# Fixed tiles given out by the plan, and a fixed order of up and down sums, in an attention and feed-forward kernel

## The chip, the cores and the metric

The kernel runs on one core of one Trainium2 chip. The metric is the device time of one execution in microseconds (us). A core has five engines that run side by side, each with its own queue in order: TensorE (PE, matmul), VectorE (DVE), ScalarE (ACT), GpSimd (POOL) and SyncE (SP, which here issues all DMAs). Matmul results land in PSUM, eight banks of 2 KB in each of 128 partitions; an engine has to read a bank out before a new sum can begin in it. The rest of the on-chip data is in SBUF.

## The reference

Talking-heads attention over 4 batches, 12 heads, 448 positions and 64 features, then a mixing layer of rank 32 and a feed-forward layer of 768 to 3072 to 768, everything in float32:

```python
scores = scale * np.matmul(q, k.transpose(0, 1, 3, 2))
scores = np.einsum('bhij,hg->bgij', scores, w_pre)
scores = scores - np.max(scores, axis=-1, keepdims=True)
attn = np.exp(scores)
attn = attn / (np.sum(attn, axis=-1, keepdims=True) + 1e-09)
attn = np.einsum('bhij,hg->bgij', attn, w_post)
x = np.matmul(attn, v)          # then [batch, position, 768]
h = xt @ U @ V                  # xt: x with position last; mixes positions
u = x + h.transpose(0, 2, 1)
out = u + np.maximum(u @ w_ch1, 0.0) @ w_ch2
```

## The kernel before

The whole program is laid out by a planner in Python, before anything runs. Each step of work is added with `plan.add` (line 107): a key, the engines that can do it with a cost in ns for each, a rank, the steps that it needs, and the slots that it holds. `Plan.order` (line 145) then plays the steps through: at each moment each idle engine takes the ready step of lowest rank whose slots are free (`pick`, line 168). A step's result counts as there after its cost and a latency (128 ns, 196 for PE). Where a step may go to several engines, the one that would end first, by costs and weights, gets it. The list that comes out is the order in which the instructions are emitted; each engine then runs its own in that order, and a framework puts in the semaphores.

Slots are of two kinds. PSUM banks are given out by the plan itself (`take`, line 137): pairs of banks for attention, single ones for up sums (`up`, at most 3), down sums (`dn`, at most 6) and the low-rank step. SBUF buffers are rings (`BUFS`, line 271): of those the plan only counts how many are left, while the tile itself is taken in turn from a pool with that many buffers (`Pool.tile`, line 75). Rings that matter here: `h` (5 slots, each one tile `hh` and one `hl`), `w0` (2) and `w1` (3) for the weights of one block, `kr` (2) for raw weights, `tmp1` and `tmp2` (1 each) for pieces being narrowed, and in attention `s`, `e`, `wr`, `st`, `q`, `x`.

Attention goes over 16 units (a batch's query groups) and 90 chunks: `qk` and its copy `s`, two `relay` DMAs that put it into the head-mixing layout `t`, `premix`, `max`, two `exp`, `eps`, `recip`, `scale`, `postmix`, its copy `a`, and `av`. Its tail overlaps the low-rank step (`tp`, `t1`, `hp`, lines 735 to 756) and the first feed-forward blocks.

The feed-forward layer goes over 24 blocks f of 128 hidden units and 4 batches b. An up sum (`up`, line 758) is 18 matmuls: six chunks, each as three products of high and low halves. ACT makes `hh` by a relu (line 769) and DVE the low part `hl` (line 773). A down sum (`down`, line 775) of one chunk c of six is 3 matmuls for each f it takes in; f are taken in pairs, so 6 matmuls: for even b the pairs end at even f, for odd b at odd f (lines 820 to 822). DVE adds it into `acc` (`gather`, line 786). The down sums of block f need the up sums of f and f-1. The ranks put up(f,b) just before the down sums of the same f and b (lines 814 to 825), but PE takes whatever is ready.

The weights come as 64-bit floats and are narrowed on chip in pieces of 384 columns, four per block (`piece`, line 587): raw load by SP, `abs` on ACT, four DVE steps (lines 615 to 625), one add on POOL (line 629), then the high half (`w0h`, `w1h`, line 310, 312 or 314) and the low half (`w0l`, `w1l`, line 317). The first steps need a `kr` and a `tmp` slot, the last two also a slot of `w0` or `w1`.

Of the kernel before, what the change touches and what calls it, by code (L numbers as in the profile page):

```python
# [23 lines left out]
NJ = 4  # L24
# [20 lines left out]
class Unit:  # L45
# [13 lines left out]
    uv=0.5, rb0=2, rb1=13.176, rbs=4, w0=4, w1=27.676, up=0.421, raw=8, x0=2.953, k0=-13.668, kstep=0.83,  # L59
# [28 lines left out]
class Plan:  # L88
# [8 lines left out]
    def __init__(self, rings, banked, banks, weight):  # L97
        self.left = dict(rings)
        self.banked, self.where = banked, {}
        self.bank_free = list(range(banks))  # L100
        self.banks = banks
        self.weight = weight
        self.steps = {}
        self.port = {}
        self.users = {}

# [30 lines left out]
    def take(self, s):  # L137
        got = self.find(s[0], self.bank_free)
        for g in got:
            self.bank_free.remove(g)  # L140
        if s[0] in PAIRS:
            self.pairs_left -= 1
        self.where[s] = got

    def order(self):
# [7 lines left out]
        held, left = set(), dict(self.left)  # L153
# [36 lines left out]
        while events:  # L190
            now = events[0][0]
            while events and events[0][0] <= now:
# [24 lines left out]
            while moved:  # L217
                moved = False
                for e in free:
# [6 lines left out]
                    engines, fn, _, _, slots = steps[k]  # L226
                    for o, _ in engines:
                        ready[o].remove(r)
                    for s in sorted(slots, key=lambda s: s[0] not in PAIRS):
                        if s not in held:  # L230
                            held.add(s)
                            if s[0] in self.banked:
                                self.take(s)
# [27 lines left out]
def build(tc, q2, kt, vj, wpre_in, wpost_in, u_in, v_in, ident, w1j, w2, out, show=None):  # L261
    nc = tc.nc
    whole, tail_ctx, mix_ctx, t_ctx, qk_ctx = (ExitStack() for _ in range(5))
    rings = {}
# [54 lines left out]
    def act(n):  # L319
        return 130 + 0.9 * n  # L320

    def dve(n):
        return 130 + 1.07 * n

    def dve_copy(n):
        return 150 + 0.53 * n
# [4 lines left out]
    def gps_copy(n):  # L331
        return 250 + 0.98 * n
# [43 lines left out]
    def buffer():  # L376
        return sb["kr"].tile([128, 2 * S], F32, "kr")

    def load_k(eng, b, p, n):
        k = tile_of(("k", b), lambda: sb["k"].tile([128, H // 2, S], F32, "k"))  # L380
        eng.dma_start(out=k[:, p:p + n], in_=kt[b, :, p:p + n])

    def load_q(eng, u, p, n, src):
        q = tile_of(("q", u), lambda: sb["q"].tile([128, H // 2, QW], F32, "q"))
# [15 lines left out]
    def qk_out(eng, u, p):  # L400
        s = T["s", u, p] = sb["s"].tile([QW, 2, S], F32, "s")
# [6 lines left out]
    for u, un in enumerate(units):  # L408
# [5 lines left out]
        for p in range(H // 2):  # L414
# [5 lines left out]
            for h in (2 * p, 2 * p + 1):  # L420
                plan.add(("relay", u, h), [("SP", (1040, 1000))], partial(relay, u=u, h=h), r + RANK["qo"], [("qk_out", u, p)], [s, ("t", u)])
# [10 lines left out]
    def neg_max(eng, k):  # L432
        mx = T["mx", k] = sb["st"].tile([128, 2], F32, "mx")
        eng.tensor_reduce(out=mx, in_=T["pre", k][:, :, :S], axis=AX.X, op=ALU.max, negate=True)  # L434

    def exp(eng, k, i):
        e = tile_of(("e", k), lambda: sb["e"].tile([128, 2, S], F32, "e"))
        sm = tile_of(("sm", k), lambda: sb["st"].tile([128, 2], F32, "sm"))
        eng.activation(out=e[:, i], in_=T["pre", k][:, i, :S], func=ACTF.Exp, bias=T["mx", k][:, i:i + 1], accum_out=sm[:, i:i + 1])  # L439

    def add_eps(eng, k):
        rc = T["rc", k] = sb["st"].tile([128, 2], F32, "rc")
# [5 lines left out]
    def scale_w(eng, k):  # L448
        wr = T["wr", k] = sb["wr"].tile([128, 2, HALF], F32, "wr")
# [17 lines left out]
    def post_out(eng, k, js):  # L467
        u, n = chunks[2 * k + js[0]]
        a = tile_of(("a", u), lambda: sb[f"a{u % 3}"].tile([128, XA, 120], F32, "a"))
# [4 lines left out]
    for k in range(NC // 2):  # L474
# [5 lines left out]
        plan.add(("max", k), [("DVE", 1080)], partial(neg_max, k=k), r + RANK["mx"], [("premix", k)], [pre, st], port=())  # L480
        for i in range(2):
            plan.add(("exp", k, i), [("ACT", 835)], partial(exp, k=k, i=i), r + RANK["ex"], [("max", k)], [pre, st, e])
        plan.add(("eps", k), [("POOL", 130)], partial(add_eps, k=k), r + RANK["ep"], [("exp", k, i) for i in range(2)], [st], port=())
        plan.add(("recip", k), [("DVE", 157)], partial(recip, k=k), r + RANK["ep"], [("eps", k)], [st], port=())
        plan.add(("scale", k), [("POOL", 420)], partial(scale_w, k=k), r + RANK["ep"], ["wpost", ("recip", k)], [st, wr], port=BOTH)
        plan.add(("postmix", k), [("PE", 825)], partial(postmix, k=k), r + RANK["post"], [("scale", k)], [e, wr, post])
        for js in ([(0, 1)] if len(us) == 1 else [(0,), (1,)]):
            u = chunks[2 * k + js[0]][0]
            plan.add(("post_out", 2 * k + js[0]), OUT_A(XA * MC * len(js)), partial(post_out, k=k, js=js), r + RANK["post"] + RANK["po"],
                     [("postmix", k)], [post, (f"a{u % 3}", u)], port=())  # L490

    def load_v(eng, b):
        v = T["v", b] = sb["vr"].tile([128, H // 2, 2, NB // 2 + 1, D], F32, "v")
# [21 lines left out]
    def av_out(eng, u, p):  # L515
        x = tile_of(("x", u), lambda: sb["x"].tile([128, H // 2, 120], F32, "x"))
# [13 lines left out]
    for u, un in enumerate(units):  # L530
        if un.gi == 0:
            plan.add(("v", un.b), [("SP", (500, 6700))], partial(load_v, b=un.b), rank_av(u, 0) - RANK["vr"], (), [("vr", un.b)])
        for p in range(0, H // 2, AV):
# [5 lines left out]
            plan.add(("av_add", u, p), [("DVE", 150 + 1.042 * AV * un.rows // 2)], partial(av_add, u=u, p=p), r + 0.65 * AV, [("av_out", u, p)], [z, x], port=())  # L539
# [47 lines left out]
    def piece(key, src, n, p, rank, finish, slots, opened, cost, early=None):  # L587
# [5 lines left out]
        def pair(n_):  # L593
            T["nx", key], T["na", key] = (sb[n_].tile([128, HW], I32, e) for e in "xa")
# [4 lines left out]
        def load_raw(eng):  # L599
            T["raw", key] = buffer()[:, :2 * HW].bitcast(I32).rearrange("p (n t) -> p n t", t=2)  # L600
            eng.dma_start(out=T["raw", key][:p, :n], in_=src)

        def narrow0(eng):
            pair("tmp1" if early else which)
# [296 lines left out]
```

## Time and profile before

| | us |
|---|---|
| median of 3 runs | 1220.93 |
| lowest, highest | 1220.0, 1221.29 |
| the profiled execution, whole | 1220.8 |
| its span, first to last instruction | 1219.0 |
| PE busy | 1096.7 (90%) |
| DVE busy | 722.7 (59%) |
| ACT busy | 377.4 (31%) |
| POOL busy | 260.8 (21%) |

Busy time is the time with at least one instruction under way on an engine. Matmuls are pipelined, so a PE that is shown busy can still have short gaps between the starts of its matmuls. "Idle before" in the rows is the time in which an engine stood still just before the instruction, with what ended it.

### The profile page before, as it was taken

The page shows a single profiled execution, that of the slowest core. Times are in us where ns is not written, and L with a number is a line of the kernel's source. Part 1 is how long each engine was busy: PE and PEld are TensorE (multiplying, and loading weights), DVE is VectorE, ACT ScalarE, POOL GpSimd, SP SyncE. Part 2 cuts the span into 40 slices and gives each one's busy share as a digit, 9 for nine tenths or more (in the row PEclk, how much of TensorE's full clock was granted, in tenths as well). Part 3 has the DMA queues.
Part 4 walks back from the last instruction along what each step waited for, and adds up shares of the span by engine and source line. Part 5 has one row for each costly group of instructions (what it writes and reads, how often), then busy time and mean ns, then how long its engine had stood idle before and what let it go on. Part 6 is the DMA issues. An engine that isn't in the chain of part 4 may idle for free.

```text
span 1219.0 us, 28556 instructions
## 1 busy us (share of the span) xinstructions
PE 1096.7 (90%) x12120; PEld 891.0 (73%) x12120; DVE 722.7 (59%) x1312; ACT 377.4 (31%) x808; POOL 260.8 (21%) x389
## 2 busy tenths in 40 slices
PE   4998889998986788899999898989999999999898
PEld 1566556655665677787878787878888787888797
DVE  0656566567666765876665655656565666655534
ACT  2766666655763232211112111111111111111100
POOL 3111111112223221331212221212222122212100
PEclk8899999989996799999999999999999999999999
DMA  7665666657665100221111121111111111111004
GB/s 267 202 192 175 195 199 191 205 178 223 186 180 173 40 1 5 76 76 52 52 39 52 40 62 42 45 47 45 47 52 52 52 52 52 44 49 52 14 1 181
DMA packets 68063, 118.52 MB, mean 97 GB/s; under 512 B 17808, under 2 KB 54112, under 8 KB 67424
## 3 DMA queue, kind: packets, MB, share of 16 engines
q1 hardware_dynamic: 67936, 116.70, 31.3%
q8 instruction: 95, 1.56, 0.5%
q14 instruction: 32, 0.26, 0.1%
HBM read 63.12 MB, written 12.28 MB: 62 GB/s over the span
## 4 chain that ended last, share of the span: by engine, by line
PE 68%; DVE 18%; DMA 5%; issue 5%; ACT 3%; SPq 1%; DVEq 0%; POOL 0%; ACTq 0%; POOLq 0%
PE bank L764 29%; PE bank L784 17%; PE bank L464 5%; DVE acc L788 5%; PE bank L429 4%; PE bank L505 4%; PE bank L398 4%; DMA t<-s 4%; DVE hl L773 2%; DVE a L620 2%; DVE a L619 2%; DVE a L615 1%; ACT hh L769 1%; DVE x L625 1%; PE bank L711 1%
## 5 line engine op out<-in xcount | busy, mean ns | idle before, releaser
L784 PE MATMUL bank<-hh,w1l 128*128 128x448 f32 x576 | 220.3, 382 | 44.0 <-DVE acc L788 42.3
L788 DVE TENSOR_TENSOR acc<-acc,bank 128x448 f32<-128x448 f32 x300 | 179.1, 616 | 74.6 <-PE bank L784 69.2
L784 PE MATMUL bank<-hl,w1h 128*128 128x448 f32 x576 | 214.6, 373 | 3.8 <-DVE hl L773 3.8
L764 PE MATMUL bank<-uh,w0l 128*128 128x448 f32 x576 | 212.7, 369 | 1.5 <-DVE acc L788 1.2
L784 PE MATMUL bank<-hh,w1h 128*128 128x448 f32 x576 | 212.3, 369 | 0.0
L764 PE MATMUL bank<-uh,w0h 128*128 128x448 f32 x576 | 211.8, 368 | 0.0
L764 PE MATMUL bank<-ul,w0h 128*128 128x448 f32 x576 | 211.8, 368 | 0.0
L769 ACT ACTIVATE hh<-bank 128x448 fp32r<-128x448 f32 x96 | 52.4, 545 | 450.4 <-PE bank L764 391.5
L773 DVE SCALAR_TENSOR_TENSOR hl<-bank,hh 128x448 fp32r<-128x448 f32 x96 | 59.7, 622 | 218.6 <-ACT hh L769 218.6
L629 POOL TENSOR_TENSOR a<-a,x 128x384 f32<-128x384 f32 (+2 forms) x99 | 99.8, 1008 | 370.0 <-DVE x L625 359.4
L784 PEld LDWEIGHTS bank<-hh,w1l 128*128 128x128 f32 x576 | 109.4, 190 | 79.0 <-DVE acc L788 61.0
L434 DVE TENSOR_REDUCE mx<-bank 128x2 f32<-128x896 f32 x90 | 97.6, 1086 | 78.9 <-PE bank L429 77.8
L464 PEld LDWEIGHTS bank<-wr,e 60*64 60x64 f32 x5040 | 92.6, 137 | 51.2 <-issue 38.1
L784 PEld LDWEIGHTS bank<-hl,w1h 128*128 128x128 f32 x576 | 109.5, 190 | 17.4 <-DVE hl L773 9.5
L764 PEld LDWEIGHTS bank<-uh,w0l 128*128 128x128 f32 x576 | 109.4, 190 | 11.5 <-DVE acc L788 1.6
L439 ACT ACTIVATE e<-bank,mx 128x448 f32<-128x448 f32 x180 | 112.9, 638 | 15.4 <-DVE rc L446 10.0
L784 PEld LDWEIGHTS bank<-hh,w1h 128*128 128x128 f32 x576 | 109.5, 190 | 8.8
L764 PEld LDWEIGHTS bank<-ul,w0h 128*128 128x128 f32 x576 | 109.3, 190 | 9.0
L398 PE MATMUL bank<-k,q 64*64 64x448 f32 (+1 forms) x768 | 99.6, 588 | 18.1 <-ACT s L310 10.7
L764 PEld LDWEIGHTS bank<-uh,w0h 128*128 128x128 f32 x576 | 109.0, 189 | 9.2
L464 PE MATMUL bank<-wr,e 60*64 60x60 f32 x5040 | 95.9, 221 | 11.9 <-issue 7.8
L429 PE MATMUL bank<-t,wpre 64*64 64x448 f32 x720 | 88.8, 559 | 9.4 <-DMA t<-s 4.7
(62 smaller groups left out, 1147.5 us busy)
## 6 DMA issues: line engine op xcount, KB each, us to landing
t<-s SPq DMA_DIRECT2D x192, 210.0 KB
kr<-in_w1j SPq DMA_DIRECT2D x48, 384.0 KB
kr<-in_w SPq DMA_DIRECT2D x48, 384.0 KB
v<-in_vj SPq DMA_DIRECT2D x4, 1536.0 KB
q<-in_q SPq DMA_DIRECT2D x32, 186.0 KB
acc<-xs SPq DMA_DIRECT2D x4, 1344.0 KB
out<-acc SPq DMA_DIRECT2D x24, 224.0 KB
xs<-x SPq DMA_DIRECT2D x10, 360.0 KB
```

Of the source, the lines that this page charges most:

```text
L398: eng.matmul(o[at, i, :S], lhsT=q[d, p, at], rhs=k[d, p, :], start=True, stop=True)
L429: eng.matmul(o[64 * j:64 * j + 64, i, :S], lhsT=wpre[64 * i:min(64 * i + 64, QW)], rhs=tt[u % 2][64 * i:min(64 * i + 64, QW), n, :], start ...
L434: eng.tensor_reduce(out=mx, in_=T["pre", k][:, :, :S], axis=AX.X, op=ALU.max, negate=True)
L439: eng.activation(out=e[:, i], in_=T["pre", k][:, i, :S], func=ACTF.Exp, bias=T["mx", k][:, i:i + 1], accum_out=sm[:, i:i + 1])
L464: eng.matmul(d, lhsT=e[64 * j:64 * j + HALF, i, x * KB:x * KB + KB], rhs=wr[64 * j:64 * j + HALF, i].rearrange("p (g m) -> p g m", m=MH), ...
L505: eng.matmul(main[i * D:(i + 1) * D, c, :n], lhsT=v[:, p + c, i, x, :], rhs=a[:, x * H + 2 * (p + c) + i, :n], start=(c == 0 and x == 0), ...
L629: eng.tensor_tensor(out=f32(a), in0=f32(a), in1=f32(x), op=ALU.add)
L764: eng.matmul(ps, lhsT=w[:, c * 128:(c + 1) * 128], rhs=u[:, c, :], start=(i == 0), stop=(i == 3 * KC - 1))
L769: eng.activation(out=hh, in_=T["up", f, b], func=ACTF.Relu)
L773: eng.scalar_tensor_tensor(out=hl, in0=T.pop(("up", f, b)), scalar=0.0, in1=f32(T["hh", f, b]), op0=ALU.max, op1=ALU.subtract)
L784: eng.matmul(ps, lhsT=w[:, cut], rhs=h, start=(i == 0), stop=(i == len(todo) - 1))
L788: eng.tensor_tensor(out=dst, in0=dst, in1=T.pop(("dn", f, b, c)), op=ALU.add)
```

## The change

Four things change.

1. A pool no longer turns through its buffers. The plan keeps a list of the free places of each ring, takes the one that came free first (`take`), and hands it back when the last user is done. `Pool.tile` makes one fixed tile for each place and returns it again whenever a step holds that place. Numbers and sizes of the buffers stay.
2. The up and down sums from block f = 2 on (`even=2`) get a fixed order, `plan.line`: one up sum, then up to three down sums from a queue, into which the six down sums of a finished f and b go behind that. `pick` passes over each step of this line that isn't next. Blocks 0 and 1 stay free.
3. Most costs of the plan are lowered, for instance `act` from 130 + 0.9 n to 57 + 0.9 n, `exp` from 835 to 622, a gather from 611 to 532, a relay on SP from 1040 to 850. `OUT_A`, a separate cost for the copy `a`, goes; `OUT` serves for both. The costs of PE's feed-forward sums stay.
4. A rank offset `ga` for gathers is added, with the value 0.

The diff, cut to its core (the helpers that name a ring's slot are changed alike at every tile):

```diff
 class Pool:
-    def __init__(self, pool):
-        self.pool = pool
-        self.n = 0
-
-    def tile(self, shape, dt, tag, **kw):
-        self.n += 1
-        return self.pool.tile(shape, dt, tag=tag, name=f"{tag}_{self.n}", **kw)
+    def __init__(self, pool, where):
+        self.pool, self.where = pool, where
+        self.made = {}
+
+    def tile(self, shape, dt, tag, slot=None):
+        at = tag if slot is None else f"{tag}_{self.where[slot]}"
+        if at not in self.made:
+            self.made[at] = self.pool.tile(shape, dt, tag=at, name=at)
+        return self.made[at]
...
     def __init__(self, rings, banked, banks, weight):
-        self.left = dict(rings)
+        self.rings = {n: list(range(c)) for n, c in rings.items()}
...
     def take(self, s):
+        if s[0] not in self.banked:
+            self.where[s] = self.rings[s[0]].pop(0)
+            return
...
+        place = {k: i for i, k in enumerate(self.line)}
+        reached = 0
+
         def pick(e):
             for r in ready[e]:
                 rank, _, k = r
+                if place.get(k, reached) != reached:
+                    continue
...
                         if s[0] in self.banked:
                             self.bank_free += self.where[s]
+                        else:
+                            self.rings[s[0]].append(self.where[s])
...
                     engines, fn, _, _, slots = steps[k]
+                    reached += k in place
...
-        sb[name] = Pool(ctx.enter_context(tc.tile_pool(name=name, bufs=bufs, side=side, **kw)))
+        sb[name] = Pool(ctx.enter_context(tc.tile_pool(name=name, bufs=1, side=side, **kw)), plan.where)
...
     def OUT(n):
-        return [("ACT", 165 + 0.833 * n), ("DVE", 150 + 1.042 * n)]
-
-    def OUT_A(n):
-        return [("ACT", 237 + 0.833 * n), ("DVE", 168 + 1.042 * n)]
+        return [("ACT", 55 + 0.833 * n), ("DVE", 75 + 1.042 * n)]
...
-                plan.add(("relay", u, h), [("SP", (1040, 1000))], partial(relay, u=u, h=h), r + RANK["qo"], [("qk_out", u, p)], [s, ("t", u)])
+                plan.add(("relay", u, h), [("SP", (850, 1000))], partial(relay, u=u, h=h), r + RANK["qo"], [("qk_out", u, p)], [s, ("t", u)])
...
-            plan.add(("exp", k, i), [("ACT", 835)], partial(exp, k=k, i=i), r + RANK["ex"], [("max", k)], [pre, st, e])
+            plan.add(("exp", k, i), [("ACT", 622)], partial(exp, k=k, i=i), r + RANK["ex"], [("max", k)], [pre, st, e])
...
-        hh = T["hh", f, b] = sb["h"].tile([128, S], F32R, "hh")
+        hh = T["hh", f, b] = sb["h"].tile([128, S], F32R, "hh", ("h", (f, b)))
...
-                plan.add(("ac", f, b, c), [("DVE", 611)], partial(gather, f=f, b=b, c=c), r + 0.01 * c, [("dn", f, b, c)] + prev, [bk])
+                plan.add(("ac", f, b, c), [("DVE", 532)], partial(gather, f=f, b=b, c=c), r + 0.01 * c - RANK["ga"], [("dn", f, b, c)] + prev, [bk])
...
+    queue, line = [], []
+    for f in range(KF):
+        for b in range(B):
+            if f >= RANK["even"]:
+                line.append(("up", f, b))
+                line += queue[:3]
+                del queue[:3]
+            if ("dn", f, b, 0) in plan.steps and f >= RANK["even"]:
+                queue += [("dn", f, b, c) for c in range(KC)]
+    line += queue
+    plan.line = line
```

## Rows read from the trace of the kernel before

**Rows 1.** The page: busy us of each engine, and the chain by engine.
```profile
PE 1096.7 (90%) x12120; PEld 891.0 (73%) x12120; DVE 722.7 (59%) x1312; ACT 377.4 (31%) x808; POOL 260.8 (21%) x389
...
PE 68%; DVE 18%; DMA 5%; issue 5%; ACT 3%; SPq 1%; DVEq 0%; POOL 0%; ACTq 0%; POOLq 0%
```

**Rows 2.** Stages: start:end, length, busy us of five engines, granted clock, DMA.
```profile
0.00:40.00 40.00, 21.71 (x180) 6.72 (x184) 4.45 (x7) 14.63 (x23) 10.44 (x10) 0.79 0.71 248
40.00:360.00 320.00, 292.94 (x8100) 195.77 (x8093) 201.50 (x333) 210.99 (x483) 60.66 (x188) 0.97 0.63 194
360.00:505.00 145.00, 115.40 (x696) 99.81 (x694) 94.62 (x168) 42.51 (x84) 37.15 (x37) 0.86 0.21 62
505.00:1160.50 655.50, 611.74 (x2881) 538.35 (x2882) 399.85 (x769) 105.45 (x214) 152.55 (x154) 0.99 0.17 49
```

**Rows 3.** Groups of 505 to 1160.5 us: busy us, mean ns, idle before, releaser.
```profile
L784 PE MATMUL bank<-hh,w1l 128*128 128x448 f32 x480 | 183.7, 383 | 40.1 <-DVE acc L788 39.6
```

**Rows 4.** The chain that ended last, in the loop: start us, us, what.
```profile
505.02 11.13 PE bank L764 x54
...
569.35 11.09 PE bank L764 x54
...
622.59 7.92 PE bank L784 x30
...
754.68 6.36 PE bank L784 x30
...
832.57 10.86 PE bank L764 x54
...
897.97 11.09 PE bank L764 x54
```

**Rows 5.** The same chain after the last weights.
```profile
1160.54 10.85 PE bank L764 x54
1171.39 7.30 PE bank L784 x36
1178.68 7.29 PE bank L764 x36
1185.98 10.95 PE bank L784 x54
```

**Rows 6.** The same chain, DVE's steps before PE goes on at 754.68.
```profile
751.61 0.56 DVE a L620
752.17 0.54 DVE hl L773
752.71 0.53 DVE acc L788
...
754.10 0.54 DVE acc L788
```

**Rows 7.** ACT's timeline: start, us, instruction, idle before it and its releaser.
```profile
839.93 0.55 ACT L769 ACTIVATE hh<-bank 128x448 fp32r<-128x448 f32 x1 [3.13 <-PE bank L764]
844.69 0.55 ACT L769 ACTIVATE hh<-bank 128x448 fp32r<-128x448 f32 x1 [4.21 <-PE bank L784]
```

**Rows 8.** SP's timeline in attention: two relays issued one behind the other.
```profile
125.88 1.60 SPq L405 DMA_DIRECT2D t<-s  x2
```

**Rows 9.** Two slices of 20 us in attention, columns as in rows 2.
```profile
200.00:220.00 20.00, 19.52 (x564) 12.76 (x558) 13.79 (x22) 13.94 (x34) 4.00 (x14) 1.00 0.70 229
...
300.00:320.00 20.00, 16.50 (x404) 11.11 (x400) 9.28 (x20) 11.31 (x26) 4.19 (x11) 0.83 0.61 184
```

**Rows 10.** The chain just before 505 us.
```profile
490.81 12.98 PE bank L784 x54
```

**Rows 11.** Timelines of DVE and POOL near 857 us.
```profile
857.59 1.18 DVE L620 SCALAR_TENSOR_TENSOR a<-x,a 128x384 f32<-128x384 f32 x1
...
857.20 1.16 POOL L317 TENSOR_TENSOR w1l<-a,w1h 128x384 fp32r<-128x384 f32 x1 [0.63 <-ACT w1h L310]
```

**Rows 12.** Waits of 505 to 1160.5 us: total, times, longest.
```profile
POOL w0h L314 <- PE bank L764: 142.6, 19, 8.5
```

More of the change, by code (lines that the diff above doesn't have):

```diff
@@ L152, in order @@
                 after.setdefault(n, []).append(k)
-        held, left = set(), dict(self.left)
+        held, left = set(), {n: len(r) for n, r in self.rings.items()}
         self.pairs_left = sum(s[0] in PAIRS for s in self.users)
@@ L483, in build @@
[L483 to L486, printed above, removed]
+            plan.add(("exp", k, i), [("ACT", 622)], partial(exp, k=k, i=i), r + RANK["ex"], [("max", k)], [pre, st, e])
@@ new lines, in build @@
+        plan.add(("eps", k), [("POOL", 120)], partial(add_eps, k=k), r + RANK["ep"], [("exp", k, i) for i in range(2)], [st], port=())
+        plan.add(("recip", k), [("DVE", 80)], partial(recip, k=k), r + RANK["ep"], [("eps", k)], [st], port=())
+        plan.add(("scale", k), [("POOL", 330)], partial(scale_w, k=k), r + RANK["ep"], ["wpost", ("recip", k)], [st, wr], port=BOTH)
+        plan.add(("postmix", k), [("PE", 815)], partial(postmix, k=k), r + RANK["post"], [("scale", k)], [e, wr, post])
@@ L538, in build @@
             plan.add(("av_out", u, p), OUT(AV * un.rows), partial(av_out, u=u, p=p), r + 0.65 * AV, [("av", u, p)], [z, x], port=())
-            plan.add(("av_add", u, p), [("DVE", 150 + 1.042 * AV * un.rows // 2)], partial(av_add, u=u, p=p), r + 0.65 * AV, [("av_out", u, p)], [z, x], port=())
+            plan.add(("av_add", u, p), [("DVE", 75 + 1.042 * AV * un.rows // 2)], partial(av_add, u=u, p=p), r + 0.65 * AV, [("av_out", u, p)], [z, x], port=())
         plan.add(("xs", u), [("SP", (460, 1650))], partial(store_x, u=u), rank_av(u, 6), [("av_add", u, p) for p in range(0, H // 2, AV)], [x])
@@ L591, in piece, with pair @@
         which = f"tmp{1 + count[0] % 2}"
-        def pair(n_):
-            T["nx", key], T["na", key] = (sb[n_].tile([128, HW], I32, e) for e in "xa")
+        def pair(slot):
+            T["nx", key], T["na", key] = (sb[slot[0]].tile([128, HW], I32, e, slot) for e in "xa")
         def get():
@@ L599, in load_raw @@
         def load_raw(eng):
-            T["raw", key] = buffer()[:, :2 * HW].bitcast(I32).rearrange("p (n t) -> p n t", t=2)
+            T["raw", key] = sb["kr"].tile([128, 2 * S], F32, "kr", raw)[:, :2 * HW].bitcast(I32).rearrange("p (n t) -> p n t", t=2)
             eng.dma_start(out=T["raw", key][:p, :n], in_=src)
         def narrow0(eng):
-            pair("tmp1" if early else which)
+            pair(first_tmp)
             raw, x, a = get()
@@ L635, in take @@
         def take(eng):
-            pair(which)
+            pair(tmp)
             eng.dma_start(out=f32(get()[2]), in_=T["nf", key][:p, :n])
@@ L741, in build @@
             plan.add(("tp", b, c), [("PE", 440)], partial(flip, b=b, c=c), r, ["ident", ("x", b)], [tp, xn])
-            plan.add(("xh", b, c), [("ACT", 593)], partial(flip_h, b=b, c=c), r, [("tp", b, c)], [tp, xn])
-            plan.add(("xl", b, c), [("DVE", 680)], partial(flip_l, b=b, c=c), r, [("xh", b, c)], [tp, xn])
+            plan.add(("xh", b, c), [("ACT", 482)], partial(flip_h, b=b, c=c), r, [("tp", b, c)], [tp, xn])
+            plan.add(("xl", b, c), [("DVE", 601)], partial(flip_l, b=b, c=c), r, [("xh", b, c)], [tp, xn])
         for k in range(KC // 2):
@@ L747, in build @@
             plan.add(("t1", b, k), [("PE", 950)], partial(by_u, b=b, k=k), r, [(("u",), 6), ("xl", b, 2 * k), ("xl", b, 2 * k + 1)], [tr, ("xn", (b, k))])
-            plan.add(("th", b, k), [("ACT", 372)], partial(t_h, b=b, k=k), r, [("t1", b, k)], [tr, t3])
-            plan.add(("tl", b, k), [("DVE", 418)], partial(t_l, b=b, k=k), r, [("th", b, k)], [tr, t3])
+            plan.add(("th", b, k), [("ACT", 272)], partial(t_h, b=b, k=k), r, [("t1", b, k)], [tr, t3])
+            plan.add(("tl", b, k), [("DVE", 336)], partial(t_l, b=b, k=k), r, [("th", b, k)], [tr, t3])
         for c in range(KC):
@@ L817, in build @@
                      [(("w", f, i), 6) for i in range(2)] + [(("ul"), b, c) for c in range(KC)], [w0, qk_])
-            plan.add(("hh", f, b), [("ACT", 545)], partial(relu_h, f=f, b=b), r - 0.4 * STEP, [("up", f, b)], [qk_, h_])
-            plan.add(("hl", f, b), [("DVE", 619)], partial(relu_l, f=f, b=b), r - 0.4 * STEP, [("hh", f, b)], [qk_, h_])
+            plan.add(("hh", f, b), [("ACT", 442)], partial(relu_h, f=f, b=b), r - 0.4 * STEP, [("up", f, b)], [qk_, h_])
+            plan.add(("hl", f, b), [("DVE", 541)], partial(relu_l, f=f, b=b), r - 0.4 * STEP, [("hh", f, b)], [qk_, h_])
             if (f - b) % 2 and f < KF - 1:
```

65 lines of the change are left out of this document (31 added, 34 removed).

## The prediction, made before the changed kernel was run

> **What bounds the kernel now.** I read the page's busy times and chain first: TensorE is busy nine tenths of the span, and the chain that ended last runs through PE for 68% and through DVE for 18% [rows 1]. So PE sets the time, and what counts is where PE is made to wait by DVE. The table of stages says which part that is [rows 2]: 0 to 40 us is start-up, 40 to 360 attention, 360 to 505 the passage (last attention work, low-rank step, the first feed-forward blocks), 505 to 1160.5 the steady feed-forward loop, over half of the span. After that come 58.5 us in which no weights are left to prepare. In the loop the granted clock is 0.99, so PE sits at its 2.4 GHz level nearly throughout; nothing is to be had from the clock there.
>
> In the loop's groups, the first matmul of a down sum is where PE stands idle: 40.1 us, nearly all put down to the DVE gather of L788, which has to empty a bank [rows 3]. That idle column is too small, because a modelled matmul end hides part of each gap. I take the loss from the chain instead. It repeats: three up sums in a row (54 matmuls) begin at 832.57 and again at 897.97 [rows 4], 65.40 us apart. Between them lie two blocks f times four batches, so 8 up sums of 18 matmuls and 24 paired down sums of 6, 288 matmuls in all. What they need is read where nobody disturbs PE: from 1160.54 to 1185.98 it issues 54 + 36 + 36 = 126 matmuls in 25.44 us, 0.2019 us each [rows 5]. So 288 need 58.15 us, and this period loses 7.25 us. Over the nine periods from 569.35 to 1160.54 [rows 4, 5] it is 591.19 - 9 x 58.15 = 67.8 us, and from 505.02 to 569.35, again 288 matmuls, 64.33 - 58.15 = 6.2 us. **Together 74 us.** Some 3.2 us of that are no wait: a run of 30 matmuls took 7.92 us where it otherwise takes 6.36 [rows 4], one of two such places. **70.8 us are waits.**
>
> Why PE waits: after three up sums in a row, downs follow in runs of up to 54 matmuls, nine down sums. A down takes PE 6 x 0.2019 = 1.21 us, and DVE needs 0.53 us for its gather [rows 6], so DVE could follow; but at that moment it also has the hl steps of the three up sums and the narrowing of weights to do, and the gather at 754.10 that lets PE go on at 754.68 stands behind those [rows 4, 6]. One cause of the crowd is the ring h: the three up sums from 832.57 are done by 843.43 [rows 4], and the hh of the third begins at 844.69, at the end of an idle of 4.21 us that a down sum ended, where the one before it, at 839.93, was let go by its up sum [rows 7]. Until hl is through, that up sum's bank is held too.
>
> **The change, part by part.**
> *Fixed MLP order.* From up(2,0) on PE runs one up sum, three downs, one up sum. In the steady state I walked the queue: for even b the downs of (f,b) come after up(f,b+2) and up(f,b+3), for odd b after the next two up sums. Each of the 80 cycles of the loop (480 leading down matmuls in [rows 3], six per cycle) is 36 matmuls, 7.27 us if PE never waits. What DVE must do in a cycle is its busy time of the stage by 80: 399.85 / 80 = 5.0 us [rows 2, 3], 69% of 7.27. Three downs arrive 1.21 us apart and then none for the 3.63 us of the up sum. Every gather, now two or three steps older than the work around it, has a lower rank than the weight pieces, so it waits at most for the step under way (narrow2, some 1.1 us as two 0.56 us instructions [rows 6]). Banks: two up sums and three downs make five of eight. So I see no bank that PE would have to wait for. A moved down sum issues no DMA; only the last ones, of f = 23, have stores behind their gathers, and these still end on one gather and one store: nil at the end.
>
> *The ring h under this order.* Its five slots are just enough. Counting holders, in half of the cycles all are held until the third down of the same cycle ends, and hh comes after that. Then hh (0.55 us [rows 7]) and hl (0.54) [rows 6] are ready about 1.2 to 2.3 us after the cycle; the shortest need for them is the first down after the next up sum, 3.63 us on. The margin is 1.3 us or more; cost nil while it lasts, and about 0.5 us in each of 40 cycles, 20 us, if DVE is later than I think.
>
> *Fixed tiles in place of rings in turn.* A new tile waits for the users of the slot that the plan saw come free, not for the oldest. Rings whose slots come free in order (e, wr, st, s, q, x) get the same tile either way: nil, with no instruction added. It matters for h, where the pairs of odd and even f free slots out of order. In turn, hh(f+1,b+1) would take the slot of (f,b), which is held long. I cost it inside the same 70.8 us (some of [rows 7] is this), not beside it.
>
> *Costs of the plan.* They change no instruction, only the order and the choice between ACT and DVE. The new values are the distance from one start to the next: a gather, 611 before and 532 now, follows the last by 0.53 us [rows 6]; a relay, 1040 before and 850 now, was issued with its neighbour in 1.60 us for both [rows 8]. The others go down in the same manner, exp from 835 to 622. So the plan's picture is nearer to the trace. But attention is re-ordered by it, and no row shows the result. The bounds: within attention the best 20 us slice has PE busy for 19.52 us and the worst for 16.50 at clock 0.83, and the mean is 292.94 / 320 x 20 = 18.3 [rows 2, 9]. Were all like the best, 320 us would become 300, a gain of 20; all like the worst, 355, a loss of 35. The passage has 29.6 us of idle at a clock of 0.86 [rows 2], so it can also go 10 either way. I take 0 for the front: PE is short of work in the rows of both kinds, and neither order is known. The gather offset ga is 0: nil.
>
> *The junction.* The burst of 54 down matmuls at 490.81 took 12.98 us [rows 10], where 54 x 0.2019 = 10.9 would do. The new order puts up sums between such downs; I take these 2 us.
>
> **The sum.** Of 70.8 us I keep back a tenth for late gathers, leaving 64; with 2 at the junction and 0 for the front, 66. Set against the profiled execution's 1220.8 us (span 1219.0, and 1.8 around it; the median of the runs is 1220.93): **1154.8, so 1155 us.** The loop period should fall from 65.2 to about 59 us.
>
> **Rivals.**
> *DVE becomes the bound.* On DVE one L620 step took 1.18 us at 857.59, where it otherwise takes 0.56, while POOL ran from 857.20 for 1.16 us [rows 6, 11]. The Trainium skill ("SBUF — State Buffer", section "Who interferes with whom") says that a DVE instruction with two SBUF inputs and a GpSimd one that reads SBUF exclude each other, and the later one waits; this row agrees. POOL is busy for 152.55 us in the loop [rows 2], 1.9 us per cycle. If all of it fell on DVE, a cycle would ask 6.9 of 7.27 us, and gathers and hl would come late. Against: 5.0 already holds today's collisions, and a gather reads one operand from PSUM. I price it, with the h margin above, at half of the waits kept: 35 us more, 1190 us.
> *The front decides.* Attention loses some 25 us by the new order (1180), or gains as much (1130).
> *Weights become the bound, and it is slower.* The fixed order no longer lets PE step around a missing piece. A pair of pieces must be done in two cycles, 14.5 us. To lose the whole 74 us over 80 cycles PE would have to wait 0.93 us per cycle, so a pair would have to take 16.4 us; above that it is slower, at 17 us some 1245 us. For it: tmp1 and tmp2 have one buffer each. Against: today finished pieces wait for PE, w0h on POOL 142.6 us in 19 times [rows 12], 7.5 us each; the supply is ahead.
> *It doesn't do what it says.* If the plan's choice of tiles gave the old turn and the order left the same bursts, the time would stay at 1221. But the 54-matmul bursts of [rows 4] cannot exist in the new order.
>
> **Chances and range.** Forecast, 1142 to 1172: 0.62. DVE bound, 1172 to 1205: 0.14. Front worse, with the loop cured: 0.08, 1172 to 1195. Front better: 0.11, 1125 to 1142. Weights, slower: 0.03. No effect: 0.02. The range of 8 in 10 is 1133 to 1192: it leaves out the slower end of the DVE case, the best of the front and the last two. A measurement here tells apart about 0.2%, 2.4 us; faster than that 0.95, within it 0.02, slower 0.03.
>
> **What would show it.** Right: in the chain PE runs 18 and 18 matmuls in turn, a period is under 60 us, the idle before L784's first matmul falls from 40 us to under 8, DVE's busy share in the loop rises to about 0.68, and ACT's hh no longer comes in groups behind bursts of up sums. Wrong in the h step: PE waits on hl L773. Wrong in the DVE step: PE waits on L788 still, with L619, L620 or L624 stretched. Wrong in the weights: PE waits before L764 on w0l. Wrong in the front: 505 us are reached at another time by more than 12 us.

## The result, and the profile after

The changed kernel takes **1182.18 us** (median of 4 runs, 1173.94 to 1189.26) against 1220.47 for the kernel before on the same chip: a ratio of 0.970, 95% interval 0.962 to 0.978. The profiled execution is the one of 1173.94 us, with a span of 1172.2 us, 46.8 less than before. One execution of e5 and one of e10 below (1143.49 and 1152.13 us) were in a slower state and are left out of the medians and ratios.

The page of the changed kernel, busy times and chain by engine, answers to [rows 1]:

```profile
PE 1069.9 (91%) x12120; PEld 887.0 (76%) x12120; DVE 734.0 (63%) x1329; ACT 372.1 (32%) x787; POOL 260.2 (22%) x393
...
PE 72%; DVE 13%; DMA 9%; ACT 3%; issue 3%; SPq 1%; POOL 0%; ACTq 0%; DVEq 0%; POOLq 0%
```

DVE's share of the chain fell from 18% to 13%, and DMA's rose from 5% to 9%. The same stages as in [rows 2]:

```profile
40.00:360.00 320.00, 290.80 (x8153) 195.73 (x8150) 182.81 (x309) 229.29 (x510) 60.06 (x189) 1.00 0.63 193
360.00:505.00 145.00, 119.92 (x745) 105.62 (x744) 99.55 (x183) 45.18 (x91) 38.43 (x37) 0.92 0.23 68
505.00:1130.00 625.00, 601.57 (x2925) 547.06 (x2924) 428.94 (x802) 82.46 (x164) 152.14 (x160) 1.00 0.18 50
```

Attention has the same picture: about 8150 matmuls in its 320 us (8100 before), PE busy 290.8 us (292.9). In the loop the share of DVE is now 428.94 / 625 = 0.69. The groups of the whole span (idle before is the last column) answer to [rows 3]:

```profile
L770 PE MATMUL bank<-uh,w0l 128*128 128x448 f32 x576 | 213.9, 371 | 22.6 <-DVE acc L794 21.3
L790 PE MATMUL bank<-hh,w1l 128*128 128x448 f32 x576 | 212.0, 368 | 6.3 <-DVE acc L794 3.4
```

The 40.1 us ahead of the first matmul of a down sum are down to 6.3. A new row has come: **the first matmul of an up sum now stands idle for 22.6 us, released by the same gather.** Where it does so is plain in the chain, of which this is one period:

```profile
725.34 3.91 PE bank L770 x18
729.26 3.65 PE bank L790 x18
...
743.80 3.66 PE bank L790 x18
747.47 0.02 issue
747.49 0.62 DVE acc L794
748.11 0.28 DVE x L630
...
749.04 3.19 DMA kr<-in_w
752.23 0.02 issue
752.25 0.36 DVE x L616
752.61 0.53 DVE acc L794
753.14 0.28 DVE a L621
753.42 0.02 issue
753.45 1.27 DVE a L625
754.71 0.03 issue
754.74 0.56 DVE a L626
755.29 0.54 DVE acc L794
755.83 0.04 issue
755.88 3.91 PE bank L770 x18
```

PE runs 18 and 18 as the order says, four times per block f, but once per block an up sum waits for a gather. A period is 755.88 - 725.34 = 30.54 us; its 144 matmuls need 144 x 0.2019 = 29.07, so 1.47 us are lost in each.

Where the 46.8 us went, by the start of a certain up sum in each trace (us from the span's start; the 17th is the first of block f = 4, the 93rd the first of f = 23):

| | before | after | change of the stretch |
|---|---|---|---|
| end of attention's last `av` | 371.0 | 370.7 | -0.3 |
| 17th up sum starts | 546.97 | 538.78 | -7.9 |
| 93rd up sum starts | 1178.52 | 1122.45 | -47.9 |
| last down sum ends | 1215.4 | 1168.5 | +9.2 |

The end is longer, since more down sums are left when the 93rd up sum starts. From the 17th up sum to the last down sum it is 668.4 before and 629.8 after, and this stretch, in which the order of up sums can't mislead, is the measure of the loop below.

### The profile page after: what moved, and what is told of

Same layout as the page of the kernel before. It is cut to its first block, busy times and chain, and to the rows that moved or that the text cites. A ratio compares the mean times of both kernels' runs of the same rounds, so it can differ in the third digit from the quotient of the medians.

```text
span 1172.2 us, 28471 instructions
## 1 busy us (share of the span) xinstructions
PE 1069.9 (91%) x12120; PEld 887.0 (76%) x12120; DVE 734.0 (63%) x1329; ACT 372.1 (32%) x787; POOL 260.2 (22%) x393
## 4 chain that ended last, share of the span: by engine, by line
PE 72%; DVE 13%; DMA 9%; ACT 3%; issue 3%; SPq 1%; POOL 0%; ACTq 0%; DVEq 0%; POOLq 0%
PE bank L770 25%; PE bank L790 24%; PE bank L470 5%; DMA kr<-in_w 5%; PE bank L404 5%; PE bank L511 5%; PE bank L435 4%; DMA t<-s 3%; DVE acc L794 3%; DVE a L625 2%; ACT e L445 2%; PE bank L717 1%; PE bank L519 1%; DVE x L631 1%; DVE a L626 1%
## 5 line engine op out<-in xcount | busy, mean ns | idle before, releaser
L770 PE MATMUL bank<-uh,w0l 128*128 128x448 f32 x576 | 213.9, 371 | 22.6 <-DVE acc L794 21.3
L790 PE MATMUL bank<-hh,w1l 128*128 128x448 f32 x576 | 212.0, 368 | 6.3 <-DVE acc L794 3.4
L790 PE MATMUL bank<-hl,w1h 128*128 128x448 f32 x576 | 210.8, 366 | 0.5 <-DVE hl L779 0.5
L770 PE MATMUL bank<-ul,w0h 128*128 128x448 f32 x576 | 211.0, 366 | 0.0
L770 PE MATMUL bank<-uh,w0h 128*128 128x448 f32 x576 | 211.0, 366 | 0.0
L635 POOL TENSOR_TENSOR a<-a,x 128x384 f32<-128x384 f32 (+2 forms) x98 | 104.0, 1061 | 478.4 <-DVE x L631 478.3
L770 PEld LDWEIGHTS bank<-uh,w0l 128*128 128x128 f32 x576 | 108.4, 188 | 39.7 <-DVE acc L794 25.9
L770 PEld LDWEIGHTS bank<-uh,w0h 128*128 128x128 f32 x576 | 108.3, 188 | 9.4
L770 PEld LDWEIGHTS bank<-ul,w0h 128*128 128x128 f32 x576 | 108.5, 188 | 8.8
L404 PE MATMUL bank<-k,q 64*60 64x448 f32 (+1 forms) x768 | 97.8, 570 | 16.4 <-ACT s L322 8.9
L322 ACT COPY s<-bank 124x896 f32<-124x896 f32 x77 | 69.7, 909 | 41.8 <-DMA t<-s 25.4
```

The lines of the kernel that those rows point to most:

```text
L322: eng.copy(out=o, in_=i)
L404: eng.matmul(o[at, i, :S], lhsT=q[d, p, at], rhs=k[d, p, :], start=True, stop=True)
L635: eng.tensor_tensor(out=f32(a), in0=f32(a), in1=f32(x), op=ALU.add)
L770: eng.matmul(ps, lhsT=w[:, c * 128:(c + 1) * 128], rhs=u[:, c, :], start=(i == 0), stop=(i == 3 * KC - 1))
L790: eng.matmul(ps, lhsT=w[:, cut], rhs=h, start=(i == 0), stop=(i == len(todo) - 1))
```

## The experiments

**What is known from the program ahead of them.** The plan gives out eight single banks, but the tiles from which they are cut are four, each of two banks (lines 289 and 293 of the changed kernel):

```python
BANKS = [sb["ps"].tile([128, 2, 512], F32, f"bank{i}") for i in range(4)]
return BANKS[w[0] // 2] if len(w) == 2 else BANKS[w[0] // 2][:, w[0] % 2]
```

The framework that puts in the semaphores looks at the tile, not at the half. In the changed program 43 up sums and 79 down sums carry a wait that names a gather of the other half of their pair, and 46 gathers one that names a down sum into the other half. A wait costs nothing where what it names is long done: with banks chosen by pairs (e5 below) 65 up sums and 198 down sums carry one, and between 560 and 1100 us none starts late. So what counts is the time. The plan tells the bank of each sum and the trace when it starts: between 560 and 1100 us 41 up and down sums of the kernel before and 19 of the changed one start more than 0.3 us after the matmul pace would let them. **Before each of these 60 a read of the pair's other half had ended 0.05 us earlier, while the sum's own half had been read out 8.7 us or more earlier.** The first four runs were made with another theory in mind (the bursts), the later ones to test this one.

All runs in one table; "loop" is from the start of the 17th up sum to the end of the last down sum, and the ratio is to the kernel before in runs on the same chip:

| run | order | costs | tiles | banks | median us | ratio, 95% | loop |
|---|---|---|---|---|---|---|---|
| before | free | old | in turn | as was | 1217 to 1221 | 1 | 668.4 |
| after | fixed | new | fixed | as was | 1182.18 | 0.970 (0.962 to 0.978) | 629.8 |
| e1_order_off | free | new | fixed | as was | 1186.12 | 0.975 (0.972 to 0.978) | 637.3 |
| e2_turn | fixed | new | in turn | as was | 1185.62 | 0.975 (0.972 to 0.979) | 631.5 |
| e3_oldcost | fixed | old | fixed | as was | 1157.44 | 0.952 (0.947 to 0.957) | 609.7 |
| e4_line_only | fixed | old | in turn | as was | 1159.65 | 0.953 (0.950 to 0.956) | 609.7 |
| e5_banks | fixed | new | fixed | by pairs | 1126.42 | 0.928 (0.922 to 0.933) | 599.0 |
| e6_abs_act | fixed | new, abs on ACT | fixed | as was | 1175.03 | 0.966 (0.961 to 0.971) | 618.5 |
| e7_before_banks | free | old | in turn | by pairs | 1123.01 | 0.923 (0.918 to 0.927) | 599.3 |
| e8_oldcost_banks | fixed | old | fixed | by pairs | 1127.43 | 0.928 (0.924 to 0.932) | 599.0 |
| e9_partner | fixed | new | fixed | half-used first | 1346.97 | 1.109 (1.104 to 1.114) | 772.9 |
| e10_free_order_banks | free | new | fixed | by pairs | 1131.87 | 0.930 (0.924 to 0.936) | 609.9 |
| e11_after_again | fixed | new | fixed | as was | 1176.11 (one run) | | 628.0 |

### Each part by itself

**The order taken back** (to the changed kernel):

```diff
-    uv=0.5, rb0=2, rb1=13.176, rbs=4, w0=4, w1=27.676, up=0.421, raw=8, even=2, ga=0, x0=2.953, k0=-13.668, kstep=0.83,
+    uv=0.5, rb0=2, rb1=13.176, rbs=4, w0=4, w1=27.676, up=0.421, raw=8, even=24, ga=0, x0=2.953, k0=-13.668, kstep=0.83,
```

> The changed kernel with the fixed order taken out: the line begins at block 24, which does not exist, so PE takes up and down sums freely again; fixed tiles and the new costs stay. Theory (the order carries the gain): the loop goes back to bursts and to about 65 us for two blocks, the whole to 1210 to 1225 us. Rival (the new costs and the fixed tiles carry it): the loop stays near 61 us for two blocks and the whole at or under 1195 us.

1186.12 us: the theory that the order does nearly all missed, and the rival held for the whole time; two blocks take 62.9 us (597.8 us over 9.5 periods), between the two. So new costs and fixed tiles without the order are worth nearly as much as all of the change, 31 of its 39 us in the loop. The waits only stand elsewhere, as the groups of this run say:

```profile
L790 PE MATMUL bank<-hh,w1l 128*128 128x448 f32 x576 | 215.4, 374 | 15.3 <-DVE acc L794 10.8 <-DVE hl L779 2.0 <-DVE acc L733 0.8
L790 PE MATMUL bank<-hl,w1h 128*128 128x448 f32 x576 | 212.9, 370 | 13.9 <-DVE hl L779 13.9
L770 PE MATMUL bank<-uh,w0l 128*128 128x448 f32 x576 | 212.5, 369 | 1.2 <-ACT xh L322 0.8 <-DVE hl L779 0.3
```

**The rings taken in turn again**, order and costs new:

```diff
     def tile(self, shape, dt, tag, slot=None):
-        at = tag if slot is None else f"{tag}_{self.where[slot]}"
-        if at not in self.made:
-            self.made[at] = self.pool.tile(shape, dt, tag=at, name=at)
-        return self.made[at]
+        self.n += 1
+        return self.pool.tile(shape, dt, tag=tag, name=f"{tag}_{self.n}")
...
-        sb[name] = Pool(ctx.enter_context(tc.tile_pool(name=name, bufs=1, side=side, **kw)), plan.where)
+        sb[name] = Pool(ctx.enter_context(tc.tile_pool(name=name, bufs=bufs, side=side, **kw)), plan.where)
```

> The changed kernel with the rings taken in turn again, the plan itself untouched: same order, same costs, only the tile that a step gets is the next of its ring. Theory (fixed tiles matter where slots come free out of order, in ring h): hh waits on down sums two cycles longer, PE waits for hl or for banks, 1195 to 1220 us. Rival (fixed tiles are without effect, the turn is nearly the plan's own): within 6 us of the changed kernel, 1174 to 1190 us.

1185.62 us, and 631.5 in the loop against 629.8 and 628.0 in the two traces of the changed kernel. The intervals overlap: fixed tiles are worth nothing that can be told from these runs, and the theory missed.

**The old costs back**, order and tiles as changed: all costs of the diff restored.

> The changed kernel with the old costs of the plan: fixed order and fixed tiles stay. Theory (order and tiles carry the gain, costs only stir the front): loop period about 61 us as in the changed kernel, whole 1170 to 1195 us. Rival (the costs are what lets DVE's order match PE): the loop period is over 63 us, the whole over 1200 us.

1157.44 us, 25 less than the changed kernel: a miss on the far side. **The new costs lose 20 us in the loop** (629.8 - 609.7). The rest lies ahead of it, where the end of attention also differs by 13 us between two executions of the same steps in the same order (364.7 in this one, 378.1 in e8_oldcost_banks), so I read nothing into it. The group that is slow after:

```profile
L773 PE MATMUL bank<-uh,w0l 128*128 128x448 f32 x576 | 213.9, 371 | 10.6 <-DVE acc L797 9.7 <-DVE acc L736 0.8
```

It is the same wait, half as long in all: in the changed kernel it comes once per block, here in each second one (18 late up sums between 560 and 1100 us there, 9 here).

**The order alone, put into the kernel before** (`plan.line`, `reached` and the test in `pick`, as in the diff of the change; nothing else of it).

> The kernel before with the fixed order alone: rings in turn and old costs. Theory (order and fixed tiles belong together): the ring h in turn holds hh back, most of the gain is lost, 1200 to 1230 us. Rival (the order alone does it): 1175 to 1190 us.

1159.65 us: nearer to the rival (1175 to 1190) than to the theory and faster than both, and the loop is 609.7 us, as with fixed tiles. So the order alone brings 58.7 us in the loop (668.4 - 609.7). With these four the sum of the parts makes no sense: order alone -59, tiles nil, costs with the order +20, costs and tiles without it 637.3 - 668.4 = -31. Parts whose worth turns its sign with another part act on something that all of them only shuffle. That is what the pairs are tested for next.

### The pairs of banks

**Banks chosen by pairs, in the changed kernel.** A single bank is taken from the pair that has been wholly free the longest; half of a pair in use only if there is no other. Nothing else is touched, and it applies only once attention has taken its last pair:

```diff
         odd = [i for i in free if i ^ 1 not in free]
+        if not self.pairs_left:
+            return sorted(free, key=lambda i: (i ^ 1 not in free,
+                max(free.index(j) for j in (i, i ^ 1) if j in free)))[:1] or None
```

> The changed kernel with another choice of bank: once attention has its last pair of banks, a single sum takes a bank whose partner in the pair is free too, the one longest free. Order, tiles and costs stay. In the changed kernel PE waits once per block f, about 1.4 us, and each time for the gather that empties the other half of the bank pair, which the framework treats as one tile. Theory (the waits that are left come from these pairs): the stretch from up sum 17 to up sum 93 falls from 584 to 553 to 562 us, the whole to 1150 to 1165 us. Rival (DVE is simply late at that point, behind the narrowing that waits for a raw load): the wait moves to another bank, the stretch stays above 575 us, the whole at 1175 to 1190.

1126.42 us; the loop came as expected (555.2 us from up sum 17 to 93), the whole is faster still because the passage gained too (the 9th up sum at 461.0, 476.4 after). Each engine has the same instructions in the same order as in the changed kernel; only the banks differ. Its groups, one row of the stages table from 560 us on, and the row of DVE's groups in the same stretch for the narrowing step that is L625 in the changed kernel:

```profile
L772 PE MATMUL bank<-uh,w0l 128*128 128x448 f32 x576 | 212.0, 368 | 0.0
...
L792 PE MATMUL bank<-hh,w1l 128*128 128x448 f32 x576 | 210.9, 366 | 0.5 <-DVE acc L796 0.4
```

```profile
560.00:1050.00 490.00, 490.00 (x2417) 453.58 (x2416) 360.63 (x675) 69.86 (x136) 118.88 (x133) 1.00 0.19 54
```

```profile
L627 DVE SCALAR_TENSOR_TENSOR a<-kr,a 128x384 int32<-128x384 int32 x68 | 49.5, 729 | 1.2
```

PE is busy in 490.00 of 490 us, with DVE at 360.63 / 490 = 0.74, more than in the changed kernel. The stretched narrowing steps are there as ever (mean 729 ns), and nobody on PE waits for them.

**The `abs` step on ACT alone, in the changed kernel.** In the chain of after the gather that PE waits for stands on DVE behind a narrowing step that waits for its raw load (749.04, 3.19 us); this takes the first such step off DVE.

```diff
-        [("ACT", 60 + 395 * s), ("DVE", 60 + 210 * s)]
+        [("ACT", 60 + 395 * s)]
```

> The changed kernel with the first narrowing step (abs) allowed on ACT alone; with the new costs the plan gives it to DVE once per block, where it waits for its raw load in front of the gathers. Theory of the bank pairs: the wait goes only where the gathers happen to move, the stretch from up sum 17 to 93 stays above 570 us. Rival (DVE's queue stands behind the load): the stretch falls to 553 to 565 us, the whole to 1150 to 1167 us.

1175.03 us, and 572.6 from up sum 17 to 93, as the theory of the pairs has it. The loop is 618.5: 11 of the 31 us that after loses against 599. The wait on the raw load is part of the reason why the gather comes late, but the stall stays, with 19.8 us before L770 instead of 22.6, half as often and longer each time.

**Banks by pairs in the kernel before**, with its free order, its old costs and its rings in turn: the same edit.

> The kernel before with the same choice of bank by free pairs and nothing else: free order, rings in turn, old costs. If the 74 us that the loop loses come from the bursts of the free order (DVE cannot empty nine down sums in a row while it does the rest), it stays at 1205 to 1220 us. If they come largely from bank pairs that are half in use, it falls to 1150 to 1185 us.

**1123.01 us, the lowest median of all (e5 and e8 can't be told from it), and 59 us faster than the changed kernel.** This decides the case: each engine still has the instructions of the kernel before in the same order, so all of the bursts that I blamed are still there.

```profile
573.98 7.28 PE bank L766 x36
581.26 14.59 PE bank L786 x72
595.85 11.09 PE bank L766 x54
606.94 7.30 PE bank L786 x36
```

72 down matmuls in a row, twelve down sums and more than the 54 that I had read, take 14.59 us, 0.2026 each: DVE follows them without PE ever waiting. The stages table from 560 us on, and the groups of the span:

```profile
560.00:1050.00 490.00, 490.00 (x2417) 453.49 (x2416) 349.26 (x636) 88.44 (x178) 122.81 (x126) 1.00 0.19 55
```

```profile
L766 PE MATMUL bank<-uh,w0l 128*128 128x448 f32 x576 | 211.7, 367 | 1.6 <-DVE acc L729 1.6
...
L786 PE MATMUL bank<-hh,w1l 128*128 128x448 f32 x576 | 210.7, 366 | 0.0
```

Where the kernel before idled 40.1 us [rows 3], it is 0.0.

**Old costs with the pairs.**

> Fixed order, fixed tiles, old costs, and the bank choice by free pairs. With the old costs the loop is already at 564 us from up sum 17 to 93 against a floor of 552.5; theory of the pairs: it falls to 553 to 558 us and the whole to 1145 to 1153 us. Rival (what is left is DVE or the clock): no change, 1153 to 1163 us.

1127.43 us, and 555.2 from up sum 17 to 93 as expected, the whole below what was expected. The loop is 599.0: the 20 us that the costs make are gone once the banks are chosen by pairs.

**The other way round: the half of a pair in use always first**, in the changed kernel.

```diff
-        if self.pairs_left and odd:
+        if odd:
             return odd[:1]
```

> The changed kernel with the suspected cause made worse: a single sum always takes a bank whose partner in the pair is in use, if there is one (a condition on attention's pairs is dropped from that rule). Order, tiles, costs stay. Theory (half-used pairs make the waits): the stretch from up sum 17 to 93 grows from 584 to over 620 us and the whole to over 1215 us, slower than the kernel before or level with it. Rival (the choice of bank matters only through how long a bank has been free): 1170 to 1195 us.

1346.97 us, 165 more than the changed kernel, with the same matmuls, order, costs and tiles. Its groups, its chain in one stretch, and the timelines of PE and DVE there:

```profile
L790 PE MATMUL bank<-hh,w1l 128*128 128x448 f32 x576 | 222.7, 387 | 97.2 <-DVE hl L779 55.7 <-DVE acc L794 37.9 <-ACT xh L322 1.9
L770 PE MATMUL bank<-uh,w0l 128*128 128x448 f32 x576 | 217.4, 378 | 61.0 <-DVE acc L794 54.5 <-DVE hl L779 5.7 <-ACT xh L322 0.7
```

```profile
727.96 0.54 DVE acc L794
728.50 0.04 issue
728.54 3.92 PE bank L770 x18
732.47 0.02 issue
732.49 0.63 DVE acc L794
733.12 0.04 issue
```

```profile
726.69 0.37 PE L790 MATMUL bank<-hh,w1h 128*128 128x448 f32 x1
...
732.49 0.62 DVE L794 TENSOR_TENSOR acc<-acc,bank 128x448 f32<-128x448 f32 x1 [4.00 <-PE bank L770]
```

Two kinds of wait are seen. The up sum at 728.54 begins when the gather of 727.96 has ended, and it goes into the half that this gather has just emptied: a real wait, since this rule hands a bank out again at once. The gather of 732.49 empties the other half of that pair, whose down sum issued its last matmul at 726.69. DVE stands idle for 4.00 us and the gather begins only when the up sum has ended, though an up sum feeds no gather: they share a tile. The next down sum, at 733.16, goes into the half that this late gather has emptied. So here the tile holds back the gather and not PE's sum: all 85 sums that start more than 0.3 us late between 560 and 1100 us waited for their own half, and the 165 us are of both kinds together. The run shows the other direction of the shared tile; what the pairs cost in the kernels before and after, e5 and e7 show.

**New costs and the free order, with the pairs.**

> New costs, fixed tiles, free order, and the bank choice by free pairs: with the three runs before it the fourth corner of order and costs once the pairs are out of the way. Theory (order and costs work on the loop only through the pairs): 1120 to 1135 us, within 8 us of the kernel with the fixed order. Rival (the fixed order has a worth of its own): over 1145 us.

1131.87 us, 5 from the kernel with the fixed order, as the theory has it. Its loop of 609.9 us is not a wait; PE is busy in 490.00 of 490 us here too. A line of its chain shows what it is:

```profile
569.71 7.43 PE bank L792 x36
```

7.43 / 36 = 0.2064 us for each matmul, where e7 had 7.30 / 36 = 0.2028 for the same 36. I come back to this below. Leaving that pace aside, all four kernels with pairs are within 599 us in the loop, whatever their order, costs and tiles: 599.0, 599.3, 599.0, and 609.9 x 0.2028 / 0.2064 = 599.3.

**The changed kernel once more**, one execution.

> The changed kernel once more, unaltered, for a second trace: its runs lay between 1174 and 1189 us. Theory (the difference between runs arises ahead of the loop, where PE's granted clock falls): the stretch from up sum 17 to 93 is again 583 to 585 us, and what differs lies before up sum 17. Rival: the loop itself differs by several us.

1176.11 us and 628.0 in the loop, where the first trace has 629.8; from up sum 17 to 93 it is 582.1, a little under what was expected. What differs more lies ahead of the loop, +3.9 at the 17th up sum.

## Why the prediction was right, and where it was not

The direction was right and the time lies in the range of 1133 to 1192, but the gain was 38 us by the medians (47 in the profiled execution) where I forecast 66, and the reason that I gave for it was not the cause. That 1182 lies in the range is in part luck: its part above 1172 was there for DVE as the bound or a worse front, and neither is what cost the time. Nor does a measurement here tell apart 2.4 us, as I wrote: the four runs of the changed kernel lie 15 us apart.

**What bounds the kernel** held: PE, made to wait by DVE, in the loop. The loss too was read well: 74 us from the chain, and in e7 choosing banks by pairs takes 668.4 - 599.3 = 69.1 us out of the loop of the kernel before, plus the passage (9th up sum at 460.5, 479.8 before).

**"Why PE waits"** is the step that failed. I put it down to bursts of down sums and a crowd of work on DVE. With the bursts kept and the banks chosen by pairs the waits are gone (e7), and with the bursts cured and the banks chosen badly the loop loses two and a half times what it did (e9: 772.9 - 599 = 174 us, 69 before), though there real waits for a bank handed out again at once are mixed in. In the kernels before and after, PE waits for gathers of a bank that it doesn't write, whose tile it shares. The crowd on DVE only sets how long such a wait lasts. The rows carried a hint that I passed over: 36 and 54 down matmuls in a row ran at 0.2028 us each, near the floor of 0.2019, after the last weights [rows 5], so a burst by itself makes no wait.

**"So I see no bank that PE would have to wait for"** is where it entered the sum. Five banks of eight are in use by that count, but there are four pairs, so a new sum can get the free half of a pair whose other half still waits for its gather. In the changed kernel this is one wait of 1.47 us per block, 28 us in 19 blocks, the main part of what is missing to the forecast: the loop lost 31 us against 599, and I had kept back 7.

**The fixed order** was priced at 64 us with what I held back. Alone it brings 58.7 us in the loop (e4), and the loop of the changed kernel without the costs is the same (e3). The size was nearly right and the mechanism was not: with the pairs out of the way order and bursts take the same time (599.0 in e8, 599.3 in e7), so what the order saves, it saves by bringing fewer sums into a pair in use (between 560 and 1100 us 41 sums start late in the kernel before, 9 in e4).

**"They change no instruction... I take 0 for the front"**: right for the front in the profile, 371.0 and 370.7 at its end, though that end moves by 13 us between executions of one plan (e3, e8); but the costs were not nil in the loop. They cost 20 us there with the order (e3 against after), and without it costs and tiles together bring 31 (e1). I had not looked for an effect on the loop at all. The effect goes through the banks, since it is nil with the pairs (e5 against e8: 599.0 both). Why the new costs meet a pair once per block, and not each second one as the old costs do, is only partly shown: the `abs` step on DVE that waits for a raw load accounts for 11 us (e6).

**The ring h and the fixed tiles**: nil was right for the ring (PE's idle ahead of the `hl` product is 0.5 us in the changed kernel, under the 20 us that I feared), and the tiles, which I left inside the 70.8 us, are nil too (e2, e4).

**The junction**: forecast -2; from the end of attention to the 17th up sum it was -7.9 (176.0 before, 168.1 after, but 172.6 in the changed kernel's second trace, so half of this belongs to the execution). With the pairs this stretch is 154.1 (e5) and 149.9 (e7), so here too the banks were the larger part.

**The rival "DVE becomes the bound"** shows its signs: PE waits for a gather, with the narrowing step L625 stretched ahead of it. The timelines of DVE and POOL there:

```profile
753.45 1.26 DVE L625 SCALAR_TENSOR_TENSOR a<-kr,a 128x384 int32<-128x384 int32 x1
754.74 0.56 DVE L626 SCALAR_TENSOR_TENSOR a<-x,a 128x384 f32<-128x384 f32 x1
```

```profile
753.07 1.22 POOL L329 TENSOR_TENSOR w0l<-a,w0h 128x384 fp32r<-128x384 f32 x1
```

The DVE step that meets POOL takes 1.26 us and the one behind it, alone, 0.56, as [rows 11] against [rows 6]. The Trainium skill's rule that the prediction weighed ("SBUF — State Buffer", section "Who interferes with whom") agrees once more. But a slow DVE is no bound here: at a higher share (0.74 against 0.69), and with such steps in it as before, PE waits for nothing in e5. The longer step only made a gather late that PE had no need to wait for.

**The rival "weights"** didn't come: between 505 and 1130 us what releases PE's up sums is the gather and nothing else (20.5 of 20.5 us of idle), and no idle time of PE there is put down to `w0h` or `w0l`.

**What was to show it**: the period was to fall under 60 us, and two blocks take 2 x 30.54 = 61.1; the idle before the first matmul of a down sum was to fall under 8 us, and it is 6.3, but another 22.6 us stand before the up sums, where I hadn't told the reader to look; DVE's share of 0.68 came as 0.69, and ACT's `hh` come one by one (at 729.35, 739.74 and 743.90 us). The sign that I named for a wrong DVE step came true, and the repair that it asks for is not on DVE.

What stays open: why the new costs' order meets a used pair once in each block (above).

## What to carry to other kernels

A planner's resource has to be the thing on which the framework makes dependencies: here eight banks were planned, four tiles were tracked, and choosing by pairs was worth 94 us of 1217 in the kernel before and 56 of 1182 in the changed one. The Trainium skill ("PSUM — Partial Sum Buffer", section "PSUM bank collisions raise a hardware error") asks for semaphores by bank or finer; a tile over two banks is guarded more coarsely than that, whether or not one wants it (no run here tried a tile for each bank). Before an order, an engine or a cost is blamed for a wait, look at which tile the waiting and the releasing instruction have in common, and run one kernel in which only the place changes and the order stays.

## What the runs showed of the hardware

A stream of float32 matmuls of 448 columns doesn't have one pace. In the profile of e10_free_order_banks PE starts one each 0.2064 us through the whole loop, in that of e7_before_banks each 0.2026 to 0.2028, both without a wait and both at a granted clock of 1.00 there. It makes 11 us of 599; the runs of one kernel differ by nearly as much (1128.8 to 1136.5 us for e10, 1123.9 to 1134.3 for e5). The single steps from one start to the next fall into two groups, up to 0.204 us and 0.205 to 0.210. Between 560 and 1050 us 2322 of e10's 2372 steps are in the slower one and 690 of e5's 2414; in the two executions of the changed kernel it is 982 of 2297 and 687 of 2304, so one kernel's mix changes from one execution to the next. In e5 every step within the up sums of the last batch is slow and none within those of the batch before it. What sets it isn't visible in the traces. The four runs of the changed kernel, 1173.94, 1181.45, 1182.90 and 1189.26 us, stand in the order of their mean granted clocks, 0.982, 0.974, 0.974 and 0.967; the one of these with a profile was the fastest, so 8 us of my 1174 against 1182 are a matter of the execution and not of the kernel.

That PE ran 490 of 490 us in e5 and e7 with DVE at 0.71 to 0.74 and POOL at 0.24 to 0.25 of the time beside it I had not expected either: I had held back time for late gathers, and with free banks there are none that count.
